# The last row's second layer norm from moments taken beside the first, in a cached attention decode with a token mixer

## The chip, the cores and the metric

The kernel runs on one core of a Trainium2 chip. The metric is device time in microseconds of one execution. Engines are named as in the profile: PE (matrix products), DVE (vector), ACT (activations), POOL (GpSimd), SP (which issues most DMAs). Each has a queue of its own and works through it in order; an instruction that waits for a semaphore holds everything behind it in its queue.

## The reference

Four rows (B = 4) of D = 512 numbers pass an attention block over a cache and a small mixer. Cut to what matters:

```python
x = A_x
mod = (_silu(c) @ w_mod).reshape(4, 6, 1, -1)
sa, ca, ga, sb, cb, gb = (mod[:, i] for i in range(6))
h = _layernorm(x) * (1 + ca) + sa
x = x + ga * _A_ref(h, k_cache, v_cache, wq, wo)   # 32 query heads, 8 key heads, 4096 cached positions
h = _layernorm(x) * (1 + cb) + sb                  # first norm of the tail
x = x + gb * _B_ref(h, w1, b1, w2, b2)             # layernorm(h) again (second norm), then
                                                   # gelu(h * w1 + b1) . w2 + b2 over F = 1792
```

So each row goes through two norms in a row: the first gives `a = (x - mean) * (1 + cb)` times a reciprocal root plus the shift `sb`, which is `h1`; the second norm of `h1` is what the mixer expands. All data are float32.

## The kernel before

The cache is read in 32 steps `i = 8 * b + h` (row b, key head h). A step's keys and values are 2 MB each. SP's queue loads them into a ring of three 4 MB buffers (`load_pair`, later `load_key` and `load_v`); a buffer is loaded again when PE has used it, so transfers are queued two to three ahead.

A step has these parts: `scores` (PE, L238), `row_max` to `copy_max` (the maximum over a row, back and forth between DVE and PE), `expo` (ACT), `turn` (DVE transposes), `values` (PE, L301), `copy_v`, `pick`, `copy_o` (to the four head vectors `oT`), `project` (PE, products with `wo`), `add_up` (DVE sum over heads). For steps 0 to 23 a Python loop sets the order; in its pass i = 22 `spread_gate` (four products of `ident`, L559, and a copy, L561) spreads the last row's gate `ga` over partitions. For the last eight steps, and for the mixer of rows 2 and 3 beside them, the order is written out by hand in the string `PLAN`, where a token is a part with its step (`v30.1`, `p31`). Nothing else reorders anything: a token that comes earlier stands earlier in the queue of every engine that it uses.

Rows 0 to 2 run their mixer (`Mixer`) beside later steps. Row 3 can't, so its way from the last values to the output is the kernel's tail:

- `f` (`fold_gate`) multiplies the `wo` of heads 6 and 7 by the gate ahead of time, one of eight pieces at a time. So `p30` and `p31` (L342) write the gated projection directly into the tile `pgx`, and `I` adds the residual part `ep` to it by a product with `ident` (L685).
- `zs`: `stats` takes `bn_stats` of 128 numbers per partition (L370) and masks them (L372); `zg`: `gather` sums them over partitions with a product of `ones` (L382); `norm` makes mean and variance (L387).
- `zm`: `adaln_last` takes the reciprocal root on ACT (L405) with one refinement on DVE, makes `h1` (L409), and takes the statistics of `h1` at once.
- `zb0`, `zb1`: `spread` spreads `h1` by four products of a column of `ident` (L417); between them stands the second `zg`.
- `zn`: `affine` makes `hb` on ACT (the spread `h1` less its mean, L425) and, on DVE, `wr` = `w1` times the second reciprocal root, by integer arithmetic and refinements (L103 to L113).
- `finish`: 14 pieces of 128 expansions, gelu and contraction (L537, L431, L542, L436), then the output.

The tokens `T2` and `T3` load ACT's tables ahead of the root and of gelu. The gate `gb` is made in the tail too (`zw`, `modmm`, L223).

Of the kernel before, what the change touches and what calls it, by code (L numbers as in the profile page):

```python
# [17 lines left out]
NF = F // 128  # L18
# [15 lines left out]
def adaln_decode(ctx: ExitStack, tc: tile.TileContext, small, x, wmod, wq, kk, kv, vv, wo, out):  # L34
# [42 lines left out]
    dv.memset(epsr[:, :, 2:3], EPS * 64)  # L77
    g32 = cst.tile([P, 32], F32, name="g32")
# [9 lines left out]
    first = g32[:, 0:1].to_broadcast([P, 32])  # L88
    QT = cst.tile([P, B, HKV, 32], F32, name="QT")
# [227 lines left out]
    ACC, OT = {}, {}  # L317

# [7 lines left out]
    def copy_o(i):  # L326
        pt = OT[i]
        OT[i] = wk.tile([P, REP], F32, name="oT")
        dv.tensor_copy(OT[i], pt)  # L329

    def project(i, pa=None):
        b, h = divmod(i, HKV)
        oT = OT.pop(i)
        if pa is None:
            pa = ps_m.tile([P, D], F32, name="pa", tag="m")
            for g in range(REP):
                mm(pa[32 * g:32 * g + 32, :], oT[:, g:g + 1].to_broadcast([P, 32]), wo_t[h][:, g, :],  # L337
                   start=True, stop=True)
        else:
            for g in range(REP):  # L340
                for c in range(4):
                    mm(pa[32 * c:32 * c + 32, :], oT[:, g:g + 1].to_broadcast([P, 32]),  # L342
                       wo_t[h][:, g, c * P:(c + 1) * P], start=(g == 0 and h == HKV - 2),
                       stop=(g == REP - 1 and h == HKV - 1))
        PA[i] = pa
# [29 lines left out]
    def gather_eps():  # L375
        pst = ps_m.tile([P, 24], F32, name="pst", tag="m")
        mm(pst, ones[0:1, :], epsr.rearrange("p a b -> p (a b)"), start=True, stop=False)
        return pst

    def gather(sm_, pst=None):  # L380
        pst = pst or gather_eps()
        mm(pst, ones, sm_.rearrange("p a b -> p (a b)"), start=False, stop=True)  # L382
        return pst
# [15 lines left out]
    def adaln_last(b, pst):  # L399
        mean, var = norm(pst)  # L400
        y = wk.tile([P, 1], F32, name="ye")
        t = wk.tile([P, 1], F32, name="te")
        a = wk.tile([P, P], F32, name="a")
        h1 = wk.tile([P, P], F32, name="h1")
        nc.scalar.activation(y, var, AF.Abs_reciprocal_sqrt, scale=1.0 / C2)  # L405
        dv.scalar_tensor_tensor(a, XK[:, b], mean, prep[:, 3], op0=OP.subtract, op1=OP.mult)
        dv.scalar_tensor_tensor(t, y, var, y, op0=OP.mult, op1=OP.mult)
        dv.scalar_tensor_tensor(y, t, 3.0 * C2, y, op0=OP.subtract, op1=OP.mult)
        dv.scalar_tensor_tensor(h1, a, y, prep[:, 2], op0=OP.mult, op1=OP.subtract)  # L409
        return h1, stats(h1, b)  # L410

    def bcast(h1, b, pb=None, cs=range(4)):
        if pb is None:
            pb = ps_e.tile([P, 4, P], F32, name="phb", tag="e")
        for c in cs:
            e = 32 * c + 8 * b
            mm(pb[:, c, :], ident[:, e:e + 1].to_broadcast([P, P]), h1, start=True, stop=True)  # L417
        return pb.rearrange("p c n -> p (c n)")
# [26 lines left out]
    class Mixer:  # L445


        def __init__(self, b):
            self.b, self.wide, self.n = b, b < B - 2, 0
            self.raw, self.done, self.ripe = [], [], 0  # L450
            self.pst = None
# [8 lines left out]
        def gather_eps(self):  # L460
            self.pst = gather_eps()

        def gather(self):
            self.st = gather(self.st, self.pst)
            self.pst = None

        def modulate(self):
            self.h1, self.st = (adaln if self.b < B - 1 else adaln_last)(self.b, self.st)

        def spread(self, pb=None, cs=range(4)):  # L470
            self.pb = bcast(self.h1, self.b, pb, cs)

        def normalise(self):
            self.hb, self.wr = affine(self.st, self.pb, w1n if self.b < B - 1 else w1)
# [89 lines left out]
    def fold_gate(gate, es):  # L564
        for e in es:
            w = wo_t[HKV - 2 + e // REP][:, e % REP]
            dv.tensor_mul(w, w, gate)
# [10 lines left out]
    for i in range(NS - HKV):  # L578
# [38 lines left out]
        if i == NS - HKV - 2:  # L617
            gate = spread_gate()

    mix, row = Mixer(B - 2), Mixer(B - 1)
# [11 lines left out]
    A29 LW f v30.1 P28 p29 g V30 t31.0 a30 x v31.0 v31.1 v31.2 P29 A30 Y y f v31.3 p30 E V31 a31 I A31 p31  # L634
    zs g zq zg T2 c zx c zm zq zb0 zc T3 zg zb1 zw0 zn zw1
# [5 lines left out]
           "N": mix.normalise, "g": mix.gelu, "c": lambda: mix.consume(1), "zc": mix.close, "zq": row.gather_eps,  # L641
           "zg": row.gather,
           "zm": row.modulate, "zn": row.normalise}
    for step in PLAN.split():
# [15 lines left out]
        elif op == "p":  # L660
            project(i, pgx[:, 4] if i >= NS - 2 else None)
# [19 lines left out]
        elif op == "E":  # L681
            ep = cst.tile([P, P], F32, name="ep")
            residual(ep, pc)
# [4 lines left out]
        elif step == "T3":  # L688
            nc.scalar.activation(tab, neg1, AF.Gelu_apprx_tanh)
        elif op == "zs":  # L690
            row.st = stats(pgx[:, 4], B - 1)
        elif op == "zx":
            dv.tensor_copy(XK[:, B - 1], pgx[:, 4])
        elif op == "zw":
            modmm(pgx[:, 0], 5, (0,) if i == 0 else (1, 2, 3))
        elif op == "zb":
            if i == 0:
                py = ps_s.tile([P, 8, P], F32, name="py3", tag="s")
            row.spread(py[:, 4:], (2 * i, 2 * i + 1))
    finish(B - 1, pgx[:, 0], py[:, 0], row.hb, row.wr)  # L700
# [34 lines left out]
```

## Time and profile before

| | us |
|---|---|
| runs: median, lowest, highest of 3 | 389.49, 388.9, 391.58 |
| the profiled execution: span from the first to the last instruction | 386.9 |
| PE, DVE, ACT busy | 298.9, 215.2, 108.0 |
| last projection (`p31`) starts | 369.61 |
| statistics of the finished row start | 370.76 |
| `h1` ready | 373.14 |
| `hb` starts, first gelu starts | 374.71, 375.83 |
| last DMA of the output is issued | 384.38 |

The profiled execution has no time beside its span; it is 2.6 us below the runs' median. In a row of the timeline the first number is the start in us from the span's start, the second the time it took; then engine, line, operation, `out<-in`, shapes and count; in brackets is how long the engine was idle before and what it waited for. A float32 product appears as two passes, so its counts are twice those of the code. 157.7 MB pass the DMA queues, 408 GB/s over the span.

### The profile page before, as it was taken

The page shows a single profiled execution, that of the slowest core. Times are in us where ns is not written, and L with a number is a line of the kernel's source. Part 1 is how long each engine was busy: PE and PEld are TensorE (multiplying, and loading weights), DVE is VectorE, ACT ScalarE, POOL GpSimd, SP SyncE. Part 2 cuts the span into 40 slices and gives each one's busy share as a digit, 9 for nine tenths or more (in the row PEclk, how much of TensorE's full clock was granted, in tenths as well). Part 3 has the DMA queues.
Part 4 walks back from the last instruction along what each step waited for, and adds up shares of the span by engine and source line. Part 5 has one row for each costly group of instructions (what it writes and reads, how often), then busy time and mean ns, then how long its engine had stood idle before and what let it go on. Part 6 is the DMA issues. An engine that isn't in the chain of part 4 may idle for free.

```text
span 386.9 us, 5714 instructions
## 1 busy us (share of the span) xinstructions
PE 298.9 (77%) x2416; PEld 122.4 (32%) x2416; DVE 215.2 (56%) x516; ACT 108.0 (28%) x132; POOL 0.7 (0%) x6
## 2 busy tenths in 40 slices
PE   0765575863966949979888859999988887999984
PEld 0111121231323313334222323443323342444562
DVE  0420351620542524676766644676875579788766
ACT  0101120110110110113567210213783104757356
POOL 0000000000000000000000000000000000000000
PEclk9998875986695775989999985978999998899999
DMA  8999999999999999999999999999999999999910
GB/s 329 430 434 434 415 451 430 410 449 432 418 447 434 430 434 432 434 432 434 426 434 429 434 429 434 434 432 434 425 434 432 434 429 434 422 427 423 404 46 3
DMA packets 7281, 157.70 MB, mean 408 GB/s; under 512 B 964, under 2 KB 980, under 8 KB 1368
## 3 DMA queue, kind: packets, MB, share of 16 engines
q1 hardware_dynamic: 7248, 157.33, 94.8%
q8 instruction: 19, 0.31, 0.3%
q14 instruction: 6, 0.05, 0.0%
q10 hardware_dynamic: 8, 0.00, 0.0%
HBM read 157.32 MB, written 0.01 MB: 407 GB/s over the span
## 4 chain that ended last, share of the span: by engine, by line
DMA 54%; PE 28%; DVE 16%; issue 1%; SPq 1%; ACTq 0%; DVEq 0%
DMA kv<-in_kv 47%; PE s L238 8%; PE pv L301 7%; DMA wq<-in_wq 6%; DVE m L243 3%; DVE p L275 3%; PE pt L324 2%; PE pa L337 2%; PE pb L258 2%; DVE uu L431 1%; DVE mx L252 1%; DVE acc L353 1%; PE qs L152 1%; PE phb L417 1%; PE pve L309 1%
## 5 line engine op out<-in xcount | busy, mean ns | idle before, releaser
L238 PE MATMUL s<-kv,QT 128*32 128x512 f32 x512 | 76.2, 715 | 35.6 <-DMA kv<-in_kv 32.6
L268 ACT ACTIVATE p<-s,nm 128x1024 f32<-128x1024 f32 x32 | 35.6, 1114 | 199.0 <-DVE nm L263 198.9
L243 DVE TENSOR_REDUCE m<-s 128x1 f32<-128x1024 f32 x32 | 39.2, 1224 | 76.1 <-PE s L238 76.0
L301 PE MATMUL pv<-kv,p 128*32 128x512 f32 x496 | 75.0, 684 | 0.4 <-DMA kv<-in_kv 0.4
L275 DVE STREAM_TRANSPOSE p<-p 128x512 f32<-128x512 f32 x64 | 41.9, 687 | 1.7 <-ACT p L268 1.7
L324 PEld LDWEIGHTS pt<-sel,po 128*128 128x128 f32 x250 | 33.6, 208 | 28.7 <-issue 15.6
L238 PEld LDWEIGHTS s<-kv,QT 128*32 128x32 f32 x512 | 16.3, 125 | 81.3 <-DMA kv<-in_kv 45.3
L337 PE MATMUL pa<-wo,oT 128*32 128x512 f32 x240 | 35.3, 663 | 4.3 <-DVE oT L329 4.2
L324 PE MATMUL pt<-sel,po 128*128 128x4 f32 x250 | 36.2, 268 | 1.4 <-DVE po L315 1.4
L315 DVE COPY po<-pv 128x512 f32<-128x512 f32 x31 | 21.4, 689 | 17.0 <-PE pv L301 17.0
L252 DVE TENSOR_REDUCE mx<-pm 1x128 f32<-1x512 f32 x32 | 21.4, 671 | 0.8 <-PE pm L247 0.7
L258 PEld LDWEIGHTS pb<-neg,mx 1*128 1x128 f32 x64 | 10.8, 210 | 32.9 <-DVE mx L252 31.1
L487 ACT ACTIVATE u<-u 128x1024 f32<-128x1024 f32 x20 | 20.4, 1052 | 2.7 <-DVE u L431 2.6
L431 DVE TENSOR_SCALAR u<-hb,wr,sm 128x512 f32<-128x512 f32 x40 | 19.9, 541 | 1.0 <-PE py L442 0.9
L353 DVE TENSOR_TENSOR acc<-acc,pa 128x512 f32<-128x512 f32 x26 | 17.7, 681 | 3.6 <-PE pa L337 3.6
L268 ACT ACT_TABLE_LOAD x11 | 14.1, 1283 | 19.0 <-DVE nm L263 18.9
L137 PE MATMUL s<-wm,sT 128*4 128x512 f32 x16 | 8.4, 684 | 12.2 <-DVE sT L123 12.2
L258 PE MATMUL pb<-neg,mx 1*128 1x1 f32 x64 | 13.5, 278 | 5.3 <-DVE mx L252 5.3
L487 ACT ACT_TABLE_LOAD x13 | 16.7, 1283 | 0.2
L247 PE MATMUL pm<-ident,m 128*1 128x128 f32 x32 | 9.1, 286 | 9.8 <-DVE rl L284 3.8
L301 PEld LDWEIGHTS pv<-kv,p 128*32 128x32 f32 x496 | 14.1, 146 | 8.1 <-issue 2.1
L247 PEld LDWEIGHTS pm<-ident,m 128*1 128x1 f32 x32 | 2.5, 80 | 39.1 <-DVE rl L284 21.0
(144 smaller groups left out, 212.3 us busy)
## 6 DMA issues: line engine op xcount, KB each, us to landing
kv<-in_kv SPq DMA_DIRECT2D x28, 4096.0 KB, 20.8
wq<-in_wq SPq DMA_DIRECT2D x2, 4096.0 KB
wo<-in_wo SPq DMA_DIRECT2D x4, 2048.0 KB
kv<-in_kv SPq DMA_DIRECT2D x4, 2048.0 KB, 18.5
wm<-in_wmod SPq DMA_DIRECT2D x2, 2048.0 KB
kv<-in_kk SPq DMA_DIRECT2D x1, 4096.0 KB
kv<-in_vv SPq DMA_DIRECT2D x3, 1024.0 KB
wm<-in_wmod SPq DMA_DIRECT2D x1, 1024.0 KB
```

Source lines behind the costliest of these rows:

```text
L238: mm(s[32 * c:32 * c + 32, n * 512:(n + 1) * 512], QT[:, b, h, :], KT[i][:, (n * 4 + c) * 512:(n * 4 + c + 1) * 512], start=True, stop=True)
L243: dv.tensor_reduce(M[i], S[i], axis=AX.X, op=OP.max)
L252: dv.tensor_reduce(mx, M[i].rearrange("o (c r) -> o r c", c=4).unsqueeze(1).to_broadcast([1, 4, 32, 4]), axis=AX.X, op=OP.max)
L258: mm(pb, M[i].rearrange("o c r -> o (c r)"), neg1, start=True, stop=True)
L268: nc.scalar.activation(p, S[i], AF.Exp, bias=M.pop(i), accum_out=l)
L275: dv.transpose(p, p)
L301: mm(PV[i][32 * q:32 * q + 32, :], pT[:, 128 * k:128 * k + 128:4], VT[i][:, 4 * k:4 * k + 4, :].rearrange("p j d -> p (j d)"), start=(k < ...
L324: mm(pt, po[:, c * DH:(c + 1) * DH], sel[:, c, :], start=(c == 0), stop=(c == n - 1))
L337: mm(pa[32 * g:32 * g + 32, :], oT[:, g:g + 1].to_broadcast([P, 32]), wo_t[h][:, g, :], start=True, stop=True)
L353: dv.tensor_add(ACC[b], ACC[b], pa)
L431: dv.tensor_scalar(u[:, e, :], hb, wr[:, j:j + 1], b1[:, j:j + 1], op0=OP.mult, op1=OP.add)
L487: nc.scalar.activation(u, u, AF.Gelu_apprx_tanh)
```

## The change

The second norm's mean and variance are no longer measured on `h1`. Since `h1 = a*y + sb` (y the first reciprocal root), they follow from moments of `a`, of `a` times the shift, and of the shift itself.

- The shift's mean `ms`, twice the centred shift `sc` and its variance plus epsilon `vs` are made once, right behind `spread_gate` in the loop's pass i = 22 (`shift_moments`: two products of one column with the constant `over`, each between DVE operations).
- The first norm's mean is made ahead of the finished row. `fold_gate` and the residual now also sum along the row (`tensor_tensor_reduce`); the mean is the sum of the residual's row sums (`zr`, a product with `less`) and of the eight head vectors `O8` times the row sums `WS` of the gated weights (`zv`, `za`). `p31` is split in two (`p31.0`, `p31.1`) with `za` between.
- `zs` (`first_moments`) centres the row with that mean: ACT squares and sums, DVE makes `a` and sums it; the sums of `a*a` and `a*sc` follow. `zq`, `zt` gather them by products.
- `zm` (`modulate_last`) takes the root, copies the moments and makes `h1`, with no statistics.
- `zb` (`spread_last`) spreads `h1` by four products that use 64 partitions each, two on the upper and two on the lower half, into two banks.
- `zn` (`normalise_last`) makes mean and variance by small DVE operations; the second reciprocal root is GpSimd's power of -0.5, and `zr2` multiplies `w1` by it. The copy `zx` and the close `zc` of row 2 now come behind it.

```diff
+    half = cst.tile([P, 1], F32, name="half")
+    dv.memset(half, -0.5)
...
+    gm = cst.tile([P, 2], F32, name="gm")
+    dv.tensor_scalar(gm[:, 0:1], g32[:, 8 * B - 8:8 * B - 7], 1.0 / D, None, op0=OP.mult)
+    dv.tensor_scalar(gm[:, 1:2], g32[:, 8 * B - 8:8 * B - 7], -1.0 / D, None, op0=OP.mult)
+    over, less = (gm[:, k:k + 1].to_broadcast([P, P]) for k in range(2))
...
+    def shift_moments():
+        s1 = wk.tile([P, 1], F32, name="s1", bufs=1)
+        dv.tensor_reduce(s1, prep[:, 2], axis=AX.X, op=OP.add)
+        p1 = ps_m.tile([P, 1], F32, name="p1", tag="m")
+        mm(p1, over, s1, start=True, stop=True)
+        LAST["ms"] = ms = cst.tile([P, 1], F32, name="ms")
+        dv.tensor_copy(ms, p1)
+        LAST["sc"] = sc = cst.tile([P, P], F32, name="sc")
+        dv.tensor_scalar(sc, prep[:, 2], ms, 2.0, op0=OP.subtract, op1=OP.mult)
+        a = wk.tile([P, P], F32, name="a")
+        dv.tensor_tensor_reduce(a, sc, sc, 0.25, 0.0, OP.mult, OP.add, s1)
+        p2 = ps_m.tile([P, 1], F32, name="p2", tag="m")
+        mm(p2, over, s1, start=True, stop=True)
+        LAST["vs"] = vs = cst.tile([P, 1], F32, name="vs")
+        dv.tensor_scalar(vs, p2, EPS, None, op0=OP.add)
+
+    def mean_rest(sep):
+        LAST["pm"] = pm = ps_m.tile([P, 1], F32, name="pmean", tag="m")
+        mm(pm, less, sep, start=True, stop=False)
+
+    def mean_dot():
+        ...
+        dv.tensor_tensor_reduce(j, O8, WS, -1.0 / D, 0.0, OP.mult, OP.add, v)
+
+    def mean_add():
+        mm(LAST["pm"], ones, LAST["v"], start=False, stop=True)
+        ...
+        dv.tensor_copy(nm, LAST["pm"])
...
+    def first_moments(xin):
+        ...
+        nc.scalar.activation(sq, xin, AF.Square, bias=nm, accum_out=st[:, 0:1])
+        dv.scalar_tensor_tensor(a, xin, nm, prep[:, 3], op0=OP.add, op1=OP.mult)
+        dv.tensor_reduce(st[:, 1:2], a, axis=AX.X, op=OP.add)
+        mm(p, over, st, start=False, stop=True)
+        ...
+        dv.tensor_tensor_reduce(j, a, LAST["sc"], 1.0, 0.0, OP.mult, OP.add, st2[:, 1:2])
+        nc.scalar.activation(sq, a, AF.Square, accum_out=st2[:, 0:1])
...
+    def modulate_last():
+        ...
+        nc.scalar.activation(y, p[:, 0:1], AF.Abs_reciprocal_sqrt, scale=1.0 / C2)
+        dv.tensor_copy(e, p)
+        dv.scalar_tensor_tensor(t, y, e[:, 0:1], y, op0=OP.mult, op1=OP.mult)
+        dv.scalar_tensor_tensor(y, t, 3.0 * C2, y, op0=OP.subtract, op1=OP.mult)
+        dv.scalar_tensor_tensor(h1, LAST["a"], y, prep[:, 2], op0=OP.mult, op1=OP.subtract)
...
+    def normalise_last(pb):
+        ...
+        dv.scalar_tensor_tensor(w, e, e, p2[:, 0:1], op0=OP.mult, op1=OP.subtract)
+        dv.scalar_tensor_tensor(t1, w, y, p2[:, 1:2], op0=OP.mult, op1=OP.add)
+        dv.scalar_tensor_tensor(var, t1, y, LAST["vs"], op0=OP.mult, op1=OP.subtract, reverse1=True)
+        nc.gpsimd.tensor_tensor(root, var, half, op=OP.pow)
+        dv.scalar_tensor_tensor(mean, e, y, LAST["ms"], op0=OP.mult, op1=OP.subtract)
+        ...
+        nc.scalar.activation(hb, pb, AF.Identity, bias=mean, scale=-1.0)
...
+    def spread_last(h1, pb):
+        e = 8 * B - 8
+        for c in (0, 2, 1, 3):
+            rows = slice(64 * (c // 2), 64 * (c // 2) + 64)
+            mm(pb[:, c // 2, c % 2, :], ident[rows, 32 * c + e:32 * c + e + 1].to_broadcast([64, P]), h1[rows],
+               start=True, stop=True)
...
-            dv.tensor_mul(w, w, gate)
+            dv.tensor_tensor_reduce(w, w, gate, 1.0, 0.0, OP.mult, OP.add, WS[:, e:e + 1])
...
             gate = spread_gate()
+            shift_moments()
...
-    A29 LW f v30.1 P28 p29 g V30 t31.0 a30 x v31.0 v31.1 v31.2 P29 A30 Y y f v31.3 p30 E V31 a31 I A31 p31
-    zs g zq zg T2 c zx c zm zq zb0 zc T3 zg zb1 zw0 zn zw1
+    A29 LW f v30.1 P28 p29 g V30 t31.0 a30 x v31.0 v31.1 v31.2 P29 A30 Y y f v31.3 p30 E V31 a31 I zr A31 zv p31.0 za p31.1
+    g T2 zq c zs zt c zm T3 zb zn zx zw zr2 zc
...
+            dv.tensor_mul(ep, pc, prep[:, 1])
+            dv.tensor_tensor_reduce(ep, ep, prep[:, 0], 1.0, 0.0, OP.add, OP.add, sep)
```

How the queues change at three places. First PE in the loop's pass i = 22, from the gate's products to the next step's scores, before:

```order
L442 MATMUL py<-u,sm 32x512 x4
L358 MATMUL pc<-yw,g_114 32x128 x4
L559 MATMUL pgb<-prep,ident 128x128 x4
L238 MATMUL s_1848<-kv,QT 32x512 x8
L324 MATMUL pt<-sel,po 128x4 x4
```

and now (`p_1858` and `p_1866` are `p1` and `p2`, `s_1856` is `s1`, `gm` holds `over`):

```order
L529 MATMUL py<-u,sm 32x512 x4
L369 MATMUL pc<-yw,g_119 32x128 x4
L641 MATMUL pgb<-prep,ident 128x128 x4
L412 MATMUL p_1858<-s_1856,gm 128x1
L420 MATMUL p_1866<-s_1856,gm 128x1
L247 MATMUL s_1872<-kv,QT 32x512 x8
L335 MATMUL pt<-sel,po 128x4 x4
```

The two products of `shift_moments` stand between the gate's products and the scores; each uses what DVE makes from the one before.

Second, PE in the tail, from the end of `p30` to the mixer's products, before:

```order
L342 MATMUL pgx<-wo_127,oT 32x128 x16
L324 MATMUL pt<-sel,po 128x4
L685 MATMUL pgx<-ep,ident 128x128
L342 MATMUL pgx<-wo_127,oT 32x128 x16
L377 MATMUL pst<-epsr,ones 128x24
L382 MATMUL pst<-stm,ones 128x24
```

and now (`v_2510` is `v8`, the eight head products; `m_2543` is `m01`, the first two moments):

```order
L353 MATMUL pgx<-wo_135,o_236 32x128 x16
L335 MATMUL pt<-sel,po 128x4
L770 MATMUL pgx<-ep,ident 128x128
L426 MATMUL pmean<-sep,gm 128x1
L353 MATMUL pgx<-wo_135,o_236 32x128 x8
L434 MATMUL pmean<-v_2510,ones 128x1
L353 MATMUL pgx<-wo_135,o_236 32x128 x8
L440 MATMUL mo<-eps_116,ones 128x2
L523 MATMUL py<-u,sm 32x128 x8
L451 MATMUL mo<-m_2543,gm 128x2
```

One product of the mean stands before the last projection and one between its halves.

Third, DVE in the tail, from the last head vector to the last piece of `wr`, with the semaphores waited for, before:

```order
L370 BN_STATS st<-pgx 128x6 [waits PE_49]
L372 TENSOR_TENSOR stm<-st,ident 128x24 [waits DVE_49]
L693 COPY xk<-pgx 128x128
L387 BN_AGGR mv<-pst 128x2 [waits PE_49]
L406 SCALAR_TENSOR_TENSOR a<-xk,mv,prep 128x128 [waits DVE_49]
L407 SCALAR_TENSOR_TENSOR te<-ye,mv 128x1 [waits Activation_49]
L408 SCALAR_TENSOR_TENSOR ye<-te,ye 128x1 [waits DVE_49]
L409 SCALAR_TENSOR_TENSOR h_2531<-a,ye,prep 128x128 [waits DVE_49]
L370 BN_STATS st<-h_2531 128x6 [waits DVE_49]
```

and now (`e_2566` is the copy of the moments, `w_2579`, `t_2580`, `v_2581` lead to the second variance):

```order
L449 SCALAR_TENSOR_TENSOR a<-pgx,nmean,prep 128x128 [waits Activation_49]
L450 TENSOR_REDUCE m_2543<-a 128x1 [waits DVE_49]
L453 ISA j,m_2544<-a,sc 128x128
L453 ISA m_2544 128x1
L469 COPY e_2566<-mo 128x2 [waits Activation_49]
L470 SCALAR_TENSOR_TENSOR te<-ye,e_2566 128x1 [waits DVE_49]
L471 SCALAR_TENSOR_TENSOR ye<-te,ye 128x1 [waits DVE_49]
L472 SCALAR_TENSOR_TENSOR h_2567<-a,ye,prep 128x128 [waits DVE_49]
L482 SCALAR_TENSOR_TENSOR w_2579<-e_2566,mo_2554 128x1 [waits PE_49]
L483 SCALAR_TENSOR_TENSOR t_2580<-w_2579,ye,mo_2554 128x1 [waits DVE_49]
L484 SCALAR_TENSOR_TENSOR v_2581<-t_2580,ye,vs 128x1 [waits DVE_49]
L486 SCALAR_TENSOR_TENSOR mean_2582<-e_2566,ye,ms 128x1
```

The statistics of the row and of `h1` are gone from DVE; `a` and the copy `e` now wait for ACT, which reads the same tile in PSUM just before, and four operations of one column stand behind `h1`. A `tensor_tensor_reduce` stands as two `ISA` rows, the second of which reads out the sum.

More of the change, by code (lines that the diff above doesn't have):

```diff
@@ L694, in adaln_decode @@
         elif op == "zw":
-            modmm(pgx[:, 0], 5, (0,) if i == 0 else (1, 2, 3))
+            modmm(pgx[:, 0], 5)
         elif op == "zb":
[L697 to L700, printed above, removed]
+            py = ps_s.tile([P, 2, 4, P], F32, name="py3", tag="s")
+            spread_last(h1, py[:, :, 2:4])
+        elif op == "zn":
+            hb, wr, root = normalise_last(py[:, :, 2:4])
+        elif step == "zr2":
+            dv.tensor_scalar(wr, w1, root, None, op0=OP.mult)
+    finish(B - 1, pgx[:, 0], py[:, 0, 0], hb, wr)
 def kernel(**inputs):
```

92 lines of the change are left out of this document (58 added, 34 removed).

## The prediction

> **What bounds the kernel now.** I read the windows of the last 30 us first, then the waits, the timeline around them, and the chain that ended last. Busy time by window (PE, weight loads, DVE, ACT, POOL, granted clock, DMA share, GB/s):
>
> ```profile
> 340.00:350.00 10.00, 9.98 (x95) 4.32 (x98) 8.90 (x18) 7.45 (x9) 0.00 (x0) 1.00 1.00 425
> 358.00:366.00 8.00, 7.97 (x76) 3.88 (x80) 5.65 (x13) 1.57 (x2) 0.00 (x0) 1.00 1.01 419
> ```
>
> The DMA engines are full to 366 us and past it; what follows is a tail of 19 us on the other engines. But PE too is idle for only 0.05 us of these 18. The waits of PE on DMA (us in total, times, longest), first in 289 to 336 us, then after 336 us, and the places of the later ones in the timeline:
>
> ```profile
> PE s L238 <- DMA kv<-in_kv: 1.3, 1, 1.3
> ```
>
> ```profile
> PE pv L301 <- DMA kv<-in_kv: 0.4, 2, 0.3
> ```
>
> ```profile
> 353.09 1.09 PE L301 MATMUL pv<-kv,p 128*32 128x512 f32 x8 [0.26 <-DMA kv<-in_kv]
> 358.03 1.95 PE L301 MATMUL pv<-kv,p 128*32 128x512 f32 x16 [0.19 <-DMA kv<-in_kv]
> 367.74 0.16 PEld L309 LDWEIGHTS pve<-kv,p 128*32 128x32 f32 x8 [0.26 <-DMA kv<-in_vv]
> ```
>
> The first of these ended at about 290 us, where that stretch begins. From there to 353.09 us PE waits for no transfer at all, and then for 0.26, 0.19 and 0.26 us. So over the last 78 us the arithmetic runs at the heels of the loads: they are late by 0.7 us in sum, and anything over 0.7 us that is added to the arithmetic after 290 us comes out at the end. The chain that ended last tells the same (start, us, what):
>
> ```profile
> 299.52 1.09 PE pgb L559 x8
> 300.61 1.90 PE s L238 x16
> ...
> 336.33 21.56 DMA kv<-in_kv
> ```
>
> From 290 to 336 us it alternates between PE and DVE. The step from 336.33 over a transfer to 358.03 is a queue, not work: the transfer waits 21.56 us behind earlier ones, so issuing it 3 us later would not land it later. The other way to 358.03 is PE's own work, which was there 0.19 us before.
>
> **The change part by part.** *The moments of the shift, at 300 us.* Before, PE goes from the gate's products (L559) straight to the next scores (L238). Now two products of one column stand between them, and each waits for DVE: gate copy, reduction, product, copy, subtraction, square with sum, read of the sum, product, then the scores. Rows for these:
>
> ```profile
> 300.64 0.69 DVE L561 COPY gate<-pgb 128x512 f32<-128x512 f32 x1 [0.70 <-PE pgb L559]
> 373.17 0.29 DVE L370 BATCH_NORM_STATS2 st<-h 128x6 f32<-128x128 f32 x1
> 373.60 0.34 DVE L507 TENSOR_SCALAR zk<-py,sm 128x128 f32<-128x128 f32 x1
> 371.33 0.40 PE L382 MATMUL pst<-stm,ones 128*128 128x24 f32 x2 [0.31 <-DVE stm L372]
> 371.77 0.27 DVE L387 BATCH_NORM_AGGREGATE mv<-pst 128x2 f32<-128x24 f32 x1 [0.29 <-PE pst L382]
> ```
>
> From the end of the gate's products: the copy 0.7, a reduction of 128 elements 0.3, the step over PE and back 0.5 (from L382's start to L387's 0.44, and 0.06 into PE), a copy of one column 0.15, the subtraction 0.3, the square with sum 0.35 and its read 0.1, into PE 0.06, the second product 0.25. That is 2.7 to 2.8 us after which the scores start; they started at once. Queued behind the two products is everything that PE does; behind them on DVE is the row maximum m, which waits for the scores. Both engines of the chain are late by the same 2.8 us. Nothing between 300 and 353 us waits for anything outside these engines, so 2.8 us reach 353 us; the three DMA waits take 0.7 of them. The net is **+2.1**. If other work covered it, the price would be 0; if each DVE step took 0.1 us more, 2.7.
>
> *The gate's fold with a sum (fold_gate).* Eight multiplications become multiplications that also sum, each with a second instruction that reads the sum:
>
> ```profile
> L567 DVE TENSOR_TENSOR wo<-wo,gate 128x512 f32<-128x512 f32 x8 | 5.4, 681 | 0.0
> 347.56 1.11 ACT L268 ACTIVATE p<-s,nm 128x1024 f32<-128x1024 f32 x1 [1.74 <-DVE nm L263]
> 348.57 0.19 ACT L268 ACTIVATION_READ_ACCUMULATOR p<-s,nm 128x1 f32 x1
> 324.39 0.60 DVE wo L567
> ```
>
> ACT's read of a sum ends 0.09 us after its operation, so 0.1 each. The chain holds two of the eight (the last row is one of them); the rest lie beside PE's work. I take **+0.2**. Bounds: 0, and 0.8 if all eight are on the path. The Trainium skill (Vector Engine (DVE) Microarchitecture Reference, Points that are easy to get wrong) says that an operation of the scalar-tensor-tensor shape with two sources in SBUF that are not bf16 runs at half rate; if the new form were one of these, each fold would be an estimated 0.5 us longer by this rule. No row of this trace has the new form.
>
> *The last projection in two halves.* PE rows of the end, and a one-column product elsewhere with what followed it:
>
> ```profile
> 369.39 0.16 DVE L329 COPY oT<-pt 128x4 f32<-128x4 f32 x1 [0.76 <-PE pt L324]
> 369.61 1.08 PE L342 MATMUL pgx<-wo,oT 128*32 128x128 f32 x32
> 370.76 0.30 DVE L370 BATCH_NORM_STATS2 st<-pgx 128x6 f32<-128x128 f32 x1 [1.20 <-PE pgx L342]
> ```
>
> ```profile
> 347.38 0.38 PE L279 MATMUL pl<-l,grp 128*128 128x1 f32 x2
> 347.62 0.27 PE L247 MATMUL pm<-ident,m 128*1 128x128 f32 x1
> ```
>
> PE went from the residual's product into the projection without a gap. Now one column product stands before it and one between its halves; each holds PE for 0.24 (347.38 to 347.62) and a bit for changing the shape of the weights. **+0.55**, bounds 0.4 and 0.8. The sum of eight products that the second one needs is made on DVE during the first half, 0.5 us, so it is hidden.
>
> *The statistics.* The steps from the finished row to the first gelu:
>
> ```profile
> 372.07 0.20 ACT L405 ACTIVATE ye<-mv 128x1 f32<-128x1 f32 x1 [3.31 <-DVE mv L387]
> 372.79 0.35 DVE L409 SCALAR_TENSOR_TENSOR h<-a,ye,prep 128x128 f32<-128x128 f32 x1
> 373.28 0.68 PE L417 MATMUL py<-h,ident 128*128 128x128 f32 x4 [0.21 <-DVE h L409]
> 373.98 0.69 PE L417 MATMUL py<-h,ident 128*128 128x128 f32 x4
> 374.71 0.69 ACT L425 ACTIVATE hb<-py,mv 128x512 f32<-128x512 f32 x1 [0.92 <-PE py L417]
> 375.83 1.52 ACT L537 ACTIVATE uu<-hb,sm,wr 128x512 f32<-128x512 f32 x2 [0.44 <-DVE wr L113]
> ```
>
> - Row to reciprocal root: 370.76 to 372.07, 1.31. Now ACT's square of 128 elements (between 0.20 for one and 0.69 for 512: 0.32) and its read 0.1; then DVE's a, which the order shows waiting for ACT since both read the same tile in PSUM, 0.35; a reduction 0.3; the product and three handovers 0.6. Together 1.65: **+0.35**. If ACT and DVE ran side by side it would be -0.1.
> - Root to h1: 1.07 before. The copy of the moments now waits for ACT's root: 0.17 more, **+0.15**.
> - h1 to hb: 373.14 to 374.71, 1.57. The second statistics leave it. What is left is the spread, 0.68 if the two half heights run side by side, 1.36 if they don't, or four small DVE operations to the mean of about 0.2 each (0.85), with 0.05 of handover: 0.9. **-0.65**; bound 0.
> - hb to the first gelu: 1.12 before, since wr came late. If wr is there first it is hb's 0.69 and a handover: **-0.4**. For that GpSimd's power has to be short: the variance is ready 0.65 after h1, two handovers and wr take 0.45, hb ends 1.63 after h1, so up to 0.5 us of power are hidden.
>
> ```profile
> L727 POOL MEMSET const-float32-1.0<- 128x1 f32 x1 | 0.1, 98 | 0.0
> masks.py:199 POOL TENSOR_SCALAR_AFFINE_SELECT ident<-ident 128x128 f32<-128x128 f32 x1 | 0.3, 292 | 0.1
> ```
>
> One column takes this engine 0.1, 128 columns 0.3. I take 0.3, nearest to the row that computes, and as upper bound 1.28 (a table load on ACT, the longest preparation that the trace shows on an engine, quoted below): 0.8 on the path. The copy of zk (0.34) now stands before DVE's expansions, but ACT has 1.52 us of gelu before it needs the first of them.
>
> **The sum.** Tail: 0.55 + 0.35 + 0.15 - 0.65 - 0.4 = 0.0. The saving is eaten by the products in the projection and by ACT's square. Stage before: 2.1 + 0.2 = 2.3. The profiled span of 386.9 becomes 389.2 us. The median shown is 389.49, 2.6 above this span; I add 2.3 to it: **391.8 us**, 0.6% slower.
>
> **The rivals.** *The delay at 300 us is absorbed.* Then only fold and tail are left: 389.5 to 389.9. The run shown spent part of its slack on a slow clock of PE:
>
> ```profile
> 322.02:325.43 3.41, 1.35 (x13) 0.21 (x5) 3.41 (x6) 0.74 (x1) 0.00 (x0) 1.00 1.00 432
> 325.43:328.84 3.41, 2.97 (x13) 1.49 (x17) 2.91 (x7) 1.32 (x2) 0.00 (x0) 0.51 0.96 413
> 328.84:332.26 3.42, 3.42 (x30) 1.49 (x26) 2.18 (x6) 3.39 (x4) 0.00 (x0) 0.50 1.00 426
> 300.54 1.92 PE L238 MATMUL s<-kv,QT 128*32 128x512 f32 x16
> 330.57 2.77 PE L238 MATMUL s<-kv,QT 128*32 128x512 f32 x16
> 344.32 1.28 ACT L676 ACT_TABLE_LOAD   x1
> ```
>
> After a stretch with 1.35 us of work PE is granted half its clock for 6.8 us, and scores take 2.77 in place of 1.92, so some 2.1 us are lost (6.8 times 1 - 1.92/2.77). An execution that escapes this has those 2.1 us in hand and takes most of the delay. Against it: the run shown did not escape. Chance 0.25.
>
> *A second slow clock.* The scores' late start leaves PE idle for 2.8 us but for two one-column products, about as long as the idle stretch before 325.43. If the clock halves there too, the scores and what follows lose the same 2.1 us: 391.8 + 2.1 = 393.9, 1.1% slower. It decides as soon as a stretch of 3.4 us holds less than about 1.4 us of PE work; at 300 us the idle time can be split over two stretches, which speaks against it. The Trainium skill (TensorE: Matmul & The Clock Gate, Part 1) puts the switch at an idle window of 3413 ns that runs free of the kernel; by this rule the phase decides, and the trace agrees with the length (325.43 to 332.26, two windows at half clock). Chance 0.22.
>
> *GpSimd's power is slow.* From 0.5 us on each us of it adds one; at 3 us the total is 394.3. For it: the engine slept since the first us. Against it: its only arithmetic took 0.3. The Trainium skill (GPSIMD Engine Reference, Instruction dispatch) names about 6 us for the first call of a freshly loaded kernel; by that rule the estimated total is over 397 us; no row here shows such a load. Chance 0.1.
>
> *The tail gains and the delay is absorbed*: if ACT and DVE share PSUM and the column products hide, 0.45 + 0.4 less: 388.7. Chance 0.05.
>
> **How the numbers follow.** The forecast has the remaining 0.38. The range, 389.2 to 394.4, runs from the absorbed case to the second slow clock; it leaves out the slowest power, the gain and some of the runs' own spread (388.9 to 391.58). A measurement of this kernel tells about 1%, 3.9 us, from no change. Faster by more would need 385.6, and the whole stretch from the row to the first gelu is 5.1 us: 0.02. Slower by more needs 393.4: the second slow clock, the slow power: 0.32. Within: 0.66.
>
> **What would show it.** Right: the two column products stand before the scores at 300 us with some 2.7 us of PE idle; PE's DMA waits after 353 us are gone; from the projection's end to the first gelu there are 4.5 us in place of 5.1. Wrong: DMA waits of 0.2 us or more still at 358 and 367 us (absorbed); a clock of 0.5 in a window after 300 us; the first gelu waiting for wr behind GpSimd.

## The result and the profile after

| | before | changed |
|---|---|---|
| runs: median, lowest, highest of 11 each | 389.49, 388.56, 391.58 | 395.05, 390.9, 398.1 |
| ratio of the times, with its 95% interval | | 1.0101 [1.0075, 1.0127] |
| profiled execution: span | 386.9 | 395.2 |

The changed kernel is slower by 1.0%, about 3.9 us (393.4 by the ratio), and its runs are spread over 7 us in place of 3. The ratio leaves out executions over 1.5% above the fastest of their kernel; here these are 5 of the 11 of the changed kernel, the profiled one (396.93 us) among them, so the profile shows more of the loss than the ratio holds.

The timeline of the changed kernel where the shift's moments stand (start, us, engine, line; in brackets the idle time and what ended it):

```profile
300.29 0.69 DVE L643 COPY gate<-pgb 128x512 f32<-128x512 f32 x1 [0.70 <-PE pgb L641]
301.23 0.38 PE L412 MATMUL p<-s,gm 128*128 128x1 f32 x2 [0.98 <-DVE s L410]
302.61 0.35 PE L420 MATMUL p<-s,gm 128*128 128x1 f32 x2 [1.00 <-DVE s L418]
302.89 2.87 PE L247 MATMUL s<-kv,QT 128*32 128x512 f32 x16
```

The gate's products start at 299.09 and the scores at 302.89: 3.80 us, where it was 1.09 before. The delay is 2.71 us. But the scores also take 2.87 in place of 1.92, and the windows say why (the first number behind the stretch is its length, then the busy time of PE, weight loads, DVE, ACT and POOL, the granted clock, the DMA share, GB/s):

```profile
300.29:303.70 3.41, 1.48 (x12) 0.88 (x16) 1.78 (x7) 0.00 (x0) 0.00 (x0) 1.00 1.02 442
303.70:314.00 10.30, 10.30 (x49) 3.63 (x41) 4.32 (x9) 1.18 (x2) 0.00 (x0) 0.50 0.97 417
334.40:341.30 6.90, 6.35 (x58) 2.71 (x54) 3.73 (x9) 6.83 (x8) 0.00 (x0) 0.51 0.91 353
365.20:368.60 3.40, 3.40 (x24) 0.67 (x16) 1.89 (x4) 1.18 (x2) 0.00 (x0) 0.50 1.01 355
382.20:385.60 3.40, 3.38 (x48) 2.39 (x48) 2.75 (x10) 2.50 (x6) 0.56 (x1) 0.51 0.02 5
```

Behind the stretch with the two waits PE has half its clock for 10.3 us, and again for 6.9, 3.4 and 3.4 us: 24 us of half clock from 300 us to the tail, where the profile of before has the one stretch of 6.8 us that the prediction shows. Over the whole execution there is no more half clock than before (the mean granted clock is 0.879, and 0.877 before); what differs is where it falls. In the second of these stretches the loads fall back too, to 353 GB/s: PE gives the buffers free late, and the two loads that SP issued at 335.57 us before (L218) it issues at 342.92 us now (L227). Of the waits of PE on DMA behind 285 us only the first of before is left:

```profile
PE s L247 <- DMA kv<-in_kv: 1.3, 1, 1.3
```

### The profile page after: what moved, and what is told of

It reads as the page before. It is cut to its first block, busy times and chain, and to the rows that moved or that the text cites. A ratio compares the mean times of both kernels' runs of the same rounds, so it can differ in the third digit from the quotient of the medians.

```text
span 395.2 us, 5756 instructions
## 1 busy us (share of the span) xinstructions
PE 300.9 (76%) x2422; PEld 123.2 (31%) x2422; DVE 216.0 (55%) x535; ACT 108.8 (28%) x136; POOL 1.3 (0%) x7
## 4 chain that ended last, share of the span: by engine, by line
DMA 42%; PE 36%; DVE 18%; issue 1%; ACT 1%; SPq 0%; ACTq 0%; DVEq 0%
DMA kv<-in_kv 41%; PE s L247 9%; PE pv L310 8%; PE pt L335 4%; PE pa L348 3%; DVE m L252 3%; DVE p L284 3%; PE qs L161 3%; PE s L146 2%; DMA sm<-in_small 2%; PE pb L267 2%; DVE mx L261 2%; DVE uu L518 1%; DVE acc L364 1%; PE pl L288 1%
## 5 line engine op out<-in xcount | busy, mean ns | idle before, releaser
L247 PE MATMUL s<-kv,QT 128*32 128x512 f32 x512 | 74.6, 703 | 43.1 <-DMA kv<-in_kv 42.5
L310 PE MATMUL pv<-kv,p 128*32 128x512 f32 x496 | 73.6, 673 | 0.0
L247 PEld LDWEIGHTS s<-kv,QT 128*32 128x32 f32 x512 | 15.5, 120 | 85.0 <-DMA kv<-in_kv 56.4
L267 PEld LDWEIGHTS pb<-neg,mx 1*128 1x128 f32 x64 | 10.0, 194 | 33.2 <-DVE mx L261 31.5
L146 PE MATMUL s<-wm,sT 128*4 128x512 f32 x16 | 9.4, 753 | 12.2 <-DVE sT L132 12.2
L267 PE MATMUL pb<-neg,mx 1*128 1x1 f32 x64 | 12.7, 265 | 5.8 <-DVE mx L261 5.7
```

The source lines that it names most:

```text
L247: mm(s[32 * c:32 * c + 32, n * 512:(n + 1) * 512], QT[:, b, h, :], KT[i][:, (n * 4 + c) * 512:(n * 4 + c + 1) * 512], start=True, stop=True)
L267: mm(pb, M[i].rearrange("o c r -> o (c r)"), neg1, start=True, stop=True)
L310: mm(PV[i][32 * q:32 * q + 32, :], pT[:, 128 * k:128 * k + 128:4], VT[i][:, 4 * k:4 * k + 4, :].rearrange("p j d -> p (j d)"), start=(k < ...
```

## The experiments

Every ratio is against the kernel before, on the same chip and in the same set of runs.

**The moments elsewhere.** The changed kernel with `shift_moments` in pass 6, where PE has waits to spare:

```diff
             gate = spread_gate()
+        if i == 6:
             shift_moments()
```

> The changed kernel with one move: the moments of the shift are made in the loop's pass 6, where PE waits for keys, and no longer in pass 22. Theory (the stall): the two column products in pass 22 hold PE and DVE for 2.5 us at the heels of the loads, and the idle time lets the clock of PE fall to half; without them the time is back at that of the kernel before, ratio 0.997 to 1.003, and no half clock follows 303 us. Rival (the tail): the loss comes from the new tail and the folds with sums; then the move changes little and the ratio stays at 1.007 to 1.013.

Measured: 389.14 us, ratio 0.9996 [0.9978, 1.0015], span 387.1. The loss is gone, as the theory of the stall has it: fold, mean, moments and tail together cost nothing that can be measured, and the place of five DVE operations and two products of one column holds the whole 1%. One half clock is left behind 303 us, of 6.8 us from 325.4 us on, where the kernel before has its own. The tail of this kernel, at full clock, in the timeline:

```profile
369.88 0.64 PE L353 MATMUL pgx<-wo,o 128*32 128x128 f32 x16
370.76 0.64 PE L353 MATMUL pgx<-wo,o 128*32 128x128 f32 x16
371.47 0.37 ACT L448 ACTIVATE sq<-pgx,nmean 128x128 f32<-128x128 f32 x1 [2.62 <-PE pgx L353]
371.96 0.35 DVE L449 SCALAR_TENSOR_TENSOR a<-pgx,nmean,prep 128x128 f32<-128x128 f32 x1 [0.94 <-ACT sq L448]
373.17 0.17 ACT L468 ACTIVATE ye<-mo 128x1 f32<-128x1 f32 x1 [0.42 <-PE mo L451]
373.38 0.16 DVE L469 COPY e<-mo 128x2 f32<-128x2 f32 x1 [0.53 <-ACT ye L468]
374.02 0.35 DVE L472 SCALAR_TENSOR_TENSOR h<-a,ye,prep 128x128 f32<-128x128 f32 x1
374.51 0.71 PE L496 MATMUL py<-h,ident 64*128 64x128 f32 x8 [0.58 <-DVE w L482]
375.08 0.56 POOL L485 TENSOR_TENSOR root<-v,half 128x1 f32<-128x1 f32 x1 [373.77 <-DVE v L484]
375.27 0.69 ACT L489 ACTIVATE hb<-py,mean 128x512 f32<-128x512 f32 x1 [0.41 <-PE py L496]
...
375.68 0.24 DVE L792 TENSOR_SCALAR wr<-sm,root 128x14 f32<-128x14 f32 x1 [0.34 <-POOL root L485]
376.00 1.52 ACT L619 ACTIVATE uu<-hb,sm,wr 128x512 f32<-128x512 f32 x2
```

From the last projection's start to the first gelu: 6.12 us, where it was 6.22 (369.61 to 375.83).

**The moments alone.** The kernel before with nothing but `shift_moments` added behind `spread_gate` in pass 22:

```diff
...
             gate = spread_gate()
+            shift_moments()
```

> The kernel before with only the moments of the shift added in pass 22; nothing uses them. The stall theory: this alone gives the loss, ratio 1.007 to 1.013, scores of pass 23 start 2.4 us after the gate's products end, and in at least some executions the half clock follows. The tail theory: ratio under 1.003.

Measured: 393.02 us, ratio 1.0055 [1.0026, 1.0083], span 394.1. The scores start 3.80 us behind the gate's products here too (299.23 to 303.03), and take even longer:

```profile
303.03 3.45 PE L242 MATMUL s<-kv,QT 128*32 128x512 f32 x16
```

So the stall alone makes the kernel slower, by less than the 0.7 to 1.3% expected. The ratio is below that of the whole change, 1.0101, though the intervals just overlap. The rest of the change is hardly the reason, since it costs nothing with the moments in pass 6. Where the half clock falls differs between the two profiles: two pieces of 3.4 us, at 303 and 313 us, here, 10.3 us there, and none here at 382 us; the pieces at 334 us (6.8 us) and 365 us (3.4 us) stand in both. That the remaining 0.5% comes from this difference is argued and not shown.

**The delay without the slow clock.** The changed kernel with two fill products, whose result nobody uses, so that PE does not idle in the stall:

```diff
         dv.tensor_reduce(s1, prep[:, 2], axis=AX.X, op=OP.add)
+        fill = ps_s.tile([P, 1024], F32, name="fill", tag="s")
+        mm(fill[:, 0:512], ident, wo_t[0][:, 0, :], start=True, stop=True)
         p1 = ps_m.tile([P, 1], F32, name="p1", tag="m")
...
         dv.tensor_tensor_reduce(a, sc, sc, 0.25, 0.0, OP.mult, OP.add, s1)
+        mm(fill[:, 512:1024], ident, wo_t[0][:, 1, :], start=True, stop=True)
```

> The changed kernel with two products of 512 columns added in pass 22, one in front of each column product of the shift's moments, so that PE works while it would wait; their result is not used. If half of the loss is the clock: the delay of 2.5 us stays, the clock stays full behind 303 us, and the ratio falls to 1.003 to 1.007. If the delay alone makes the loss: ratio 1.008 to 1.013 as for the changed kernel. If neither (tail): unchanged too, with the half clock gone.

Measured: 390.83 us, ratio 1.0025 [1.0005, 1.0045], a little under the 1.003 to 1.007 expected, span 388.8. PE does more work than in the changed kernel, in the same time to the scores, and the kernel is faster by 0.75%. The stretch at the stall and PE's rows of this kernel:

```profile
300.00:303.41 3.41, 3.26 (x19) 1.32 (x21) 1.79 (x7) 0.00 (x0) 0.00 (x0) 1.00 0.91 394
```

```profile
302.89 1.92 PE L247 MATMUL s<-kv,QT 128*32 128x512 f32 x16
...
355.01 1.04 PE L310 MATMUL pv<-kv,p 128*32 128x512 f32 x8
...
363.56 1.95 PE L310 MATMUL pv<-kv,p 128*32 128x512 f32 x16
...
371.04 0.64 PE L353 MATMUL pgx<-wo,o 128*32 128x128 f32 x16
...
375.69 1.22 PE L499 MATMUL py<-h,ident 64*128 64x128 f32 x8 [0.58 <-DVE w L485]
```

and the same places with the moments in pass 6, whose scores start at 300.27:

```profile
353.18 1.09 PE L310 MATMUL pv<-kv,p 128*32 128x512 f32 x8 [0.52 <-DMA kv<-in_kv]
...
358.11 1.95 PE L310 MATMUL pv<-kv,p 128*32 128x512 f32 x16 [0.18 <-DMA kv<-in_kv]
...
361.85 2.14 PE L310 MATMUL pv<-kv,p 128*32 128x512 f32 x16
362.89 0.21 PEld L310 LDWEIGHTS pv<-kv,p 128*32 128x32 f32 x8 [0.83 <-DMA kv<-in_vv]
```

The scores have their full clock (1.92). The delay shrinks on its way: 2.62 us at the scores, 1.83 at 355, 1.71 at 363.6, 1.16 at the last projection. So 1.46 us are made up. PE's listed waits on DMA are only a part of it (0.52 and 0.18 us): the values at 361.85 take 2.14 with loads still landing and 1.95 without. That wait lies inside a group of products; it stands with the weight loads (PEld, 0.83 us at 362.89) and not with PE. The half clock is not gone altogether: 6.8 us are left from 327.9 us on, where the kernel with the moments in pass 6 has its own from 325.4, and 3.4 us from 375.6, in the tail, where the spread of `h1` takes 1.22 us for 0.71. So about 0.5 us of this kernel's loss is still clock.

**The fold alone.** The kernel before with the summing form in `fold_gate`:

```diff
-            dv.tensor_mul(w, w, gate)
+            dv.tensor_tensor_reduce(w, w, gate, 1.0, 0.0, OP.mult, OP.add, WS[:, e:e + 1])
```

> The kernel before with only the fold of the gate made to sum as well (eight operations with a read of the sum each; the sums are not used). The stall theory has 0.0 to 0.2 us for it: ratio 0.999 to 1.002. The fold as cause: 1.005 or more, with folds clearly longer than 0.68 us.

Measured: 389.44 us, ratio 1.0003 [0.9978, 1.0028]. Its group of instructions (us in all, mean ns of one):

```profile
L568 DVE CUSTOM_DVE_ANT_0 wo<-wo,gate 128x512 f32<-128x512 f32 x8 | 5.4, 680 | 0.0
```

680 ns, where the plain product took 681; the read of the sum (0.08) starts before the operation ends. The fold adds nothing.

**ACT and DVE on one PSUM tile.** The moments in pass 6, and the tail's two turns on a tile taken apart: DVE makes `a` before ACT squares, the moment of the mean gets a product and tile of its own, `te` reads PSUM itself. That one engine waits for the other is a semaphore wait that stands in the program.

```diff
-        nc.scalar.activation(sq, xin, AF.Square, bias=nm, accum_out=st[:, 0:1])
         dv.scalar_tensor_tensor(a, xin, nm, prep[:, 3], op0=OP.add, op1=OP.mult)
+        nc.scalar.activation(sq, xin, AF.Square, bias=nm, accum_out=st[:, 0:1])
         dv.tensor_reduce(st[:, 1:2], a, axis=AX.X, op=OP.add)
+        pe = ps_m.tile([P, 1], F32, name="pe1", tag="m")
+        mm(pe, over, st[:, 1:2], start=True, stop=True)
...
+        dv.tensor_copy(e, pe)
...
-        dv.tensor_copy(e, p)
-        dv.scalar_tensor_tensor(t, y, e[:, 0:1], y, op0=OP.mult, op1=OP.mult)
+        dv.scalar_tensor_tensor(t, p[:, 0:1], y, y, op0=OP.mult, op1=OP.mult)
```

> The changed kernel with the shift's moments made in pass 6, and the tail's two waits of DVE for ACT on the same PSUM tile turned round or taken away: DVE makes a before ACT squares the row, the moment of the mean gets a product and a tile of its own (copied beside ACT's root), and te reads the root's moment in PSUM. Theory (ACT and DVE take turns on a PSUM tile, and that is on the path): the row's end to the root falls from 1.70 to 1.35 us, the root to h1 from 1.20 to 1.0, all else as with the moments in pass 6: about 388.6 us, ratio 0.9985 to 0.999. Rival (the turns only trade places, ACT's square now waits for DVE and ends as late): row to root 1.65 to 1.75, ratio as with the moments in pass 6 (0.9996). Rival (the tail's gain goes to waits for the loads): not possible here, since nothing in the tail waits for a load.

Measured: 388.78 us (lowest 388.12), ratio 0.9994 [0.9978, 1.0009], span 386.9.

```profile
371.75 0.35 DVE L448 SCALAR_TENSOR_TENSOR a<-pgx,nmean,prep 128x128 f32<-128x128 f32 x1 [0.45 <-PE pgx L353]
372.14 0.37 ACT L449 ACTIVATE sq<-pgx,nmean 128x128 f32<-128x128 f32 x1 [3.01 <-DVE a L448]
...
373.14 0.17 ACT L471 ACTIVATE ye<-mo 128x1 f32<-128x1 f32 x1
...
373.79 0.35 DVE L474 SCALAR_TENSOR_TENSOR h<-a,ye,prep 128x128 f32<-128x128 f32 x1
...
375.76 1.52 ACT L621 ACTIVATE uu<-hb,sm,wr 128x512 f32<-128x512 f32 x2
```

In the profile the theory holds: row to root 1.39 (1.70 before this edit), root to the end of `h1` 1.00 (1.20), row to gelu 4.01 (4.53). Half a microsecond is 0.13% of the time and within the ratio's interval. In its profiled execution the loads landed 0.3 us later (values at 353.46), so the last projection starts at 370.15 and the span is only 0.2 us shorter. This is the fastest version of the changed kernel; that it beats the kernel before is not shown.

**GpSimd's power twice.** The moments in pass 6, and a second power in a row:

```diff
-        nc.gpsimd.tensor_tensor(root, var, half, op=OP.pow)
...
+        nc.gpsimd.tensor_tensor(half_root, var, half, op=OP.pow)
+        nc.gpsimd.tensor_tensor(root, half_root, ones[:, 0:1], op=OP.pow)
```

> The changed kernel with the shift's moments in pass 6, and GpSimd's power done twice in a row (the second to the power of 1, so the result is the same). Theory (the power is only just hidden: wr is ready 0.08 us before hb is): all of the second power and its handover comes out at the end, 0.55 to 0.65 us; hb's start to the first gelu rises from 0.73 to 1.3. Rival (there are 0.2 us in reserve, as the prediction had it): 0.35. Rival (the first call of the engine carries a cost of its own): the second power takes 0.1 to 0.3 and 0.2 us come out.

Measured: 389.63 us, ratio 1.0009 [0.9987, 1.0031].

```profile
375.22 0.55 POOL L486 TENSOR_TENSOR hroot<-v,half 128x1 f32<-128x1 f32 x1 [373.91 <-DVE v L484]
375.41 0.69 ACT L491 ACTIVATE hb<-py,mean 128x512 f32<-128x512 f32 x1 [0.41 <-PE py L498]
375.86 0.55 POOL L487 TENSOR_TENSOR root<-hroot,ones 128x1 f32<-128x1 f32 x1
...
376.76 1.52 ACT L621 ACTIVATE uu<-hb,sm,wr 128x512 f32<-128x512 f32 x2 [0.67 <-DVE wr L794]
```

`hb` to gelu is 1.35 for 0.73: 0.62 us come out, and gelu now waits for `wr`. The single power was hidden with next to nothing to spare. First and second call take the same 0.55.

**The spread over full height.** The moments in pass 6, and products over 128 partitions:

```diff
-            rows = slice(64 * (c // 2), 64 * (c // 2) + 64)
-            mm(pb[:, c // 2, c % 2, :], ident[rows, 32 * c + e:32 * c + e + 1].to_broadcast([64, P]), h1[rows],
+            mm(pb[:, c // 2, c % 2, :], ident[:, 32 * c + e:32 * c + e + 1].to_broadcast([P, P]), h1,
```

> The changed kernel with the shift's moments in pass 6, and the spread of h1 with products over all 128 partitions in place of two half heights side by side; all else as there. Theory (the half heights run in pairs side by side): the spread's four products take 1.3 to 1.4 us in place of 0.71, h1 to hb 1.45 to 1.55 in place of 0.90, +0.55 to 0.6 us at the end. Rival (the mean, made by four DVE operations, is what hb waits for): +0.3 or less. Rival (half heights bring nothing): same.

Measured: 390.05 us, ratio 1.0017 [1.0002, 1.0033].

```profile
374.67 1.13 PE L495 MATMUL py<-h,ident 128*128 128x128 f32 x8 [0.59 <-DVE w L482]
...
375.83 0.69 ACT L489 ACTIVATE hb<-py,mean 128x512 f32<-128x512 f32 x1 [0.83 <-PE py L495]
```

1.13 us for 0.71, and `hb` 0.41 us later. The theory of the half heights side by side has the sign and the mechanism; the size is less than its 0.55, because four full products into two banks take 1.13 and not 1.36.

**One fill product.** The changed kernel with the first of the two fills alone (the first `+` lines above).

> The changed kernel as it is, with the shift's moments at 300 us, and one fill product of 128x512 (nobody uses its result) ahead of the first column product; before the second PE idles as in the changed kernel. PE works some 2.5 us of 300.0 to 303.5 in place of 1.5 (3.35 with two fills). Theory (the half clock follows a stretch of 3.41 us with less than about 1.4 us of work): no half clock behind 300 us, scores in 1.92, and the time of two fills, 390.8 us, ratio 1.0025. Rival (any idle of 1 us at this place is enough): scores in 2.8 to 3.5 us, ratio 1.005 to 1.01 as with none.

Measured: 390.91 us, ratio 1.0050 [1.0023, 1.0078]; four of its 11 runs took 393.2 to 393.3, the profiled one (span 391.4) among them. Its windows:

```profile
299.90:303.31 3.41, 2.29 (x15) 1.31 (x17) 1.77 (x7) 0.00 (x0) 0.00 (x0) 1.00 0.93 404
358.09:361.50 3.41, 3.31 (x42) 2.50 (x42) 2.46 (x9) 2.36 (x3) 0.00 (x0) 1.00 1.00 424
361.50:365.00 3.50, 3.50 (x24) 0.68 (x16) 1.90 (x4) 1.19 (x2) 0.00 (x0) 0.51 1.02 417
```

At the stall one fill is enough: 2.29 us of work, no half clock behind it, scores in 1.92. But half clocks come later, at 330.8 us, at 361.5 and in the tail; the one at 361.5 follows a stretch in which PE counts as busy for 3.31 of 3.41 us. The median is the theory's 390.8, the ratio is twice what it expected, with an interval that just holds it, and the rule of 1.4 us of work does not hold.

**PE work taken away.** The moments in pass 6, and the gate's spread left out: GpSimd fills the gate with ones, so the last row is not gated. PE has 1.1 us less to do at 300 us.

```diff
-            mm(pgb[:, c, :], ident[:, e:e + 1].to_broadcast([P, P]), prep[:, 1], start=True, stop=True)
...
-        dv.tensor_copy(gate, pgb.rearrange("p c n -> p (c n)"))
+        nc.gpsimd.memset(gate, 1.0)
```

> The changed kernel with the shift's moments in pass 6, and without the spread of the gate in pass 22: the gate's four products and the copy are left out, GpSimd fills the gate with ones (so the last row is not gated by its gate). This takes 1.1 us from PE and 0.7 from DVE at 300 us. Theory (PE runs at the heels of the loads): PE's waits for the loads after 336 us grow by about what PE gains, from 0.9 us to 1.7 or 2, the last projection starts less than 0.4 us earlier (369.5 or later), and the ratio stays within 0.998 to 1.0. Rival (the arithmetic is the bound, and the loads only follow): the last projection starts 1.0 us earlier, at 368.9, ratio 0.9965 to 0.9975.

PE's waits on DMA from 294 us, and its last projection:

```profile
PE pv L310 <- DMA kv<-in_kv: 1.5, 3, 0.9
PE s L247 <- DMA kv<-in_kv: 0.2, 1, 0.2
```

```profile
369.77 0.64 PE L353 MATMUL pgx<-wo,o 128*32 128x128 f32 x16
```

The waits are 1.7 us (0.7 listed in this view with the gate's products), and the last projection starts 0.11 us earlier: in this profile less work behind 300 us brings next to nothing, as the theory of the loads' heels says. The time missed the expectation: 390.54 us, ratio 1.0036 [1.0008, 1.0064], with runs from 388.77 to 393.53. The profiled execution is the fastest of them, so what the others lost has no profile and stays open.

**Half the stall.** The moments in pass 6, and in pass 22 a dummy of the first half: a fill product, the reduction, the first column product.

```diff
             gate = spread_gate()
...
+            mm(fill[:, 0:512], ident, wo_t[0][:, 0, :], start=True, stop=True)
...
+            dv.tensor_reduce(s1, prep[:, 2], axis=AX.X, op=OP.add)
...
+            mm(p1, over, s1, start=True, stop=True)
```

> The changed kernel with the shift's moments in pass 6, and in pass 22 a dummy of the first half of that stall: one fill product, the reduction of the shift on DVE and the first column product that waits for it (results unused). The scores start some 1.2 us later (301.5 in place of 300.27), at full clock. Theory from the run with two fills, where 1.46 of 2.62 us were made up before the last projection: all of the 1.2 us are made up, the waits for the loads after 336 us are gone or under 0.3, the last projection starts at 369.7 to 370.1, ratio 0.999 to 1.001. Rival (the prediction's step: only the 0.7 us of waits that the trace shows can be made up): the last projection starts 0.5 us later, at 370.4, ratio 1.001 to 1.0015.

```profile
301.85 1.92 PE L247 MATMUL s<-kv,QT 128*32 128x512 f32 x16
...
370.40 0.64 PE L353 MATMUL pgx<-wo,o 128*32 128x128 f32 x16
```

Measured: 389.43 us (388.87 to 389.72), ratio 0.9994 [0.9977, 1.0010]. The gate's products start at 299.41 here, against 299.19 with the moments in pass 6 alone, so the scores are 1.36 us late by themselves and the last projection 0.30: 1.06 us are made up, between the 0.7 of the prediction and the 1.46 above. The profile lands on the rival's 370.4, the ratio on the theory's, so the run does not decide between the two. How much can be made up seems to differ from execution to execution with the landing of the loads: PE waits 0.52 us at 353 us with the moments in pass 6, and 0.93 in the kernel with the tail's turns taken apart.

## Why the prediction was right or wrong

The forecast was 391.8 us, a loss of 0.6%. The ratio puts the result at 393.4, within the range, and the median of all 11 runs, 395.05, lies above it. The sign held, and so did the place: with the moments in pass 6 the loss is gone. The likeliest case did not come: it was the rival of the second slow clock. That the number came as near as it did is partly luck: the net delay was forecast about 1 us too long, and the clock, forecast at nothing, cost about 3 us. Of the signs named, PE's waits behind 353 us are gone, as the likeliest case had it, and the clock of 0.5 behind 300 us is the sign against it.

- **The delay, 2.7 to 2.8 us:** 2.71, and 2.71 in the kernel with the moments alone (3.80 less 1.09). The sum of prices from rows of before held.
- **What is made up, 0.7 us:** 1.1 to 1.5. The step took three listed waits as the whole slack and left out what a weight load waits inside a group of products. The net is not +2.1 but about +1.1 us by the ratios (1.0025 less 0.9996), +1.7 by the medians (390.83 less 389.14); in the profile some 0.5 us of it is clock in the tail. The profile of before has the wait that was left out, longer than the 0.7 us of the three together:

```profile
362.79 0.21 PEld L301 LDWEIGHTS pv<-kv,p 128*32 128x32 f32 x8 [0.80 <-DMA kv<-in_vv]
```

- **No second slow clock, "the idle time can be split over two stretches":** this step failed. The stall fell into one stretch of 3.41 us, its 1.48 us of work were few enough, and the half clock held for three stretches, not two, with more of it at 334, 365 and 382 us. By the ratios it costs 0.76%, 3.0 us (1.0101 less 1.0025); the rival had 2.1 and took it for a single event. The limit of about 1.4 us of work that the rival went by did not hold either: 1.48 was too few here, and 3.31 in the kernel with one fill.
- **The fold, +0.2:** 0. The summing form takes 680 ns where the plain product took 681. It shows nothing of the half rate that the Trainium skill (Vector Engine (DVE) Microarchitecture Reference, Points that are easy to get wrong) gives for a scalar-tensor-tensor shape with two SBUF sources that are not bf16; whether this form counts as that shape no run shows.
- **The projection in halves, +0.55:** row ready 1.59 us after the start of the projection in place of 1.15, and the start itself 0.12 later behind the residual's product: 0.56.
- **Row to root, +0.35; root to h1, +0.15; h1 to hb, -0.65; hb to gelu, -0.4:** +0.39, +0.13, -0.67, -0.39. The sum, 0.0, is what the profile of the kernel with the moments in pass 6 shows, 8.11 us from the last values to gelu for 8.09. That ACT and DVE take turns on a PSUM tile, by the program's waits, and that this is on the path, is shown by the kernel that turns them round.
- **GpSimd's power, 0.3 with 0.5 hidden:** 0.56. The value was too small, and all of it was still hidden: `wr` is ready at 375.92 and `hb` at 375.96. The doubled power comes out in full. No run shows the first-call load of some 6 us that the Trainium skill (GPSIMD Engine Reference, Instruction dispatch) names.
- **The arithmetic at the heels of the loads:** the profiles agree with it from both sides, by the filled stall (the delay shrinks as the waits go) and by the gate left out (the waits grow, the last projection stays). The times of the kernel without the gate do not: they came out 0.4% longer, and why is open.

## What to carry to other kernels

Put work whose inputs are ready early where the engines wait for transfers anyway; a chain that crosses from DVE to PE twice stops everything behind it in PE's queue for the whole chain, whatever its operations take. Where PE idles for two to three microseconds in the middle of dense work, price the clock as well as the delay: here it cost about three times as much by the ratios, and one product of 128x512 that nobody uses kept the clock at that place. The list of PE's waits gives the least slack that there is; for the rest read the waits of the weight loads, and compare how long the same group of products takes with and without loads landing.

## What the runs showed of the hardware

Half clock came in pieces of 3.4 us (10.3, 6.9, 3.4, 3.4). The length is that of the window of 3413 ns that the Trainium skill gives (TensorE: Matmul & The Clock Gate, Part 1), but "idle" as the busy column has it does not decide: half clock followed stretches with 1.48 us of work, and one with 3.31 of 3.41. In that last one 14 of the 42 products have one or four columns, and the other 28 use 32 of the array's 128 columns of weights, so PE is busy with little for the array to do.

The records show more. Within each trace every change of the clock up to the last products lies on one grid of 3.413 us; in the changed kernel it changes at 303.73, 313.97, 334.45, 341.28, 365.17, 368.58 and 382.24 us. Cut the trace on this grid, and count in each window, for every product of the profile, its moving columns times the share of the 128x128 array that its weights fill (a product of 512 columns with 32 columns of weights counts 128). The window of the changed kernel's stall, 300.32 to 303.73 us, then holds 803 such columns, the like one with one fill 1666, and with two 2812; the one with 3.31 us of busy time holds 1341. From 290 to 382 us the 12 traces of this case have 311 whole windows. The 34 that a half clock follows hold at most 1341, but for one with 1492; the 277 that a full clock follows hold 1406 or more. The busy times of the two kinds overlap from 1.71 to 3.41 us. So in these traces it is the work in the array that tells the two kinds apart, with a limit near 1400. The limit was read off these windows afterwards, from products whose ends the profile models, and no run was made to try it. It would also say why the start of a stretch matters: the kernel with two fills runs the products of that 3.31 us stretch at 357.7 to 359.8 us and keeps its clock, because its grid parts them between windows with 2438 and 2451.

Two products of 64 partitions each run side by side: four took 0.71 us, four of 128 partitions 1.13. GpSimd's power of one column takes 0.55 us, first call or second.
